# Attention scores from 64-row products: two heads side by side on the array, keys held without their zero blocks

## The chip, the cores and the metric

The kernel runs on one core of a Trainium2 chip. The metric is the device time of one execution in microseconds (us). A core has five engines that run at the same time and wait for each other through semaphores: TensorE (PE in the profile; its weight loads are listed apart as PEld), VectorE (DVE), ScalarE (ACT), GpSimd (POOL) and SyncE (SP, which here only issues DMAs).

## What is computed

The inputs are float32. The first half is an attention whose keys and values are first averaged over groups of 8 positions; the second half is a feed-forward block with an unusual activation over all 4608 positions.

```python
# q, k, v: (8 batches, 8 heads, 576 positions, 64)
k_p = k.reshape(B, H, 72, 8, 64).mean(axis=3)          # 72 pooled keys
v_p = v.reshape(B, H, 72, 8, 64).mean(axis=3)
scores = (1 / 8) * np.matmul(q, k_p.transpose(0, 1, 3, 2))
scores = scores - scores.max(axis=-1, keepdims=True)
attn = np.exp(scores); attn = attn / (attn.sum(-1, keepdims=True) + 1e-9)
x = np.matmul(attn, v_p)                               # heads joined: (4608, 512)
h = x @ w_in                                           # (4608, 2048)
sp = np.maximum(h, 0) + np.log1p(np.exp(-np.abs(h)))
out = (h * erf(sp)) @ w_out                            # (4608, 512)
```

## The kernel before, in words

**The work.** The 4608 rows of `x` are cut into 9 chunks (`ck`) of 512, and the feed-forward block runs chunk by chunk: products with `w_in` (L1004 for chunks 0 and 1, L948 with seven half-size products for the others), the activation on ACT and DVE, and products with `w_out` (L1062). These two lines and L948 are most of the kernel. The attention of a batch (`job`) is put between them, so that a chunk's rows of `x` are ready when the chunk starts.

**Attention of a batch.** The pooled keys of the four pairs of heads come into a tile `ks` (128 partitions x 4 pairs x 72): partitions 0 to 63 hold the channels of one head of a pair, partitions 64 to 127 those of the other. In batches 1 to 7 two ACT instructions (L654) copy them, with a factor of -1/64, into `kbd`, which has 144 columns for a pair: 72 of one head with zeros in the other head's rows, then 72 of the other. The zeros come from one memset at the start (L465). Batch 0 has a tile of its own for this, `kb0`.

**A full tile** (`softmax_tile`) is 128 queries of all 8 heads; a batch from 1 to 7 has 4 of them, 28 in all. The queries lie in `raw` as 128 partitions (two heads' channels) x 4 pairs x 128. Its scores are four products (L718), in two groups of two: the queries of a pair are the stationary operand (128 rows x 128 columns), `kbd` of that pair is the moving one (144 columns). Each group has a PSUM bank of its own. DVE then takes the extreme and subtracts it, ACT takes the exponential (as a sigmoid with a bias, so that the activation table of the feed-forward block serves), DVE and POOL normalise, TensorE turns the tile (L774, and L788 for the part that goes over 128), ACT and DVE split it into a high and a low part, and the products with the values follow (L898).

**A half tile** (`half_tile`) is what 576 leaves over: 64 queries, one for each of batches 1 to 7. Its four products (L821) have a stationary operand of 128 rows x 64 columns; two of them write partitions 0 to 63 of the bank and two write 64 to 127, one after the other in turn, so that each takes one half of the array's columns. It has the same chain behind it as a full tile, with L850 and L858 for the turning.

**The order.** Every operation is entered in a small planner (`Program`) with an engine, a cost in ns, a due time and the tiles that it reads and writes. The planner runs through them greedily and writes each engine's instructions in the order that it finds; for the start of the kernel a table (`FIRST`) gives the order by hand, as a list of operation numbers. Costs and due times set only the order: on the chip each engine takes its own list in sequence and waits on semaphores. The scores of a tile have a cost of 2 x 250 for each group, those of a half tile 2 x 250.

Of the kernel before, what the change touches and what calls it, by code (L numbers as in the profile page):

```python
# [11 lines left out]
F32 = mybir.dt.float32  # L12
# [8 lines left out]
POOL = 8  # L21
# [52 lines left out]
HALF_SCORES = 2  # L74
# [109 lines left out]
D137 A377 A376 A104 G142 G132 P1745 P407 P404 P1751 D345 D105 P1752 G385 D346 D108 D111 D405 P1753 P1746 P1747 A149 A141 A138 A148 A156 S380 S196 S168  # L184
S175 S382 S182 S549 S545 G386 G347 D408 D143 D406 P1754 P348 D409 D144 G139 G387 G389 P1755 P350 P1748 P426 P1756 D381 D427 A163 A349 A351 A410 D411
G145 G146 D428 A1757 D412 P358 P352 P1769 P1770 P1771 P355 P1772 G393 D150 D413 A353 A359 A356 D354 D360 D357 D151 G390 G414 G415 P1773 P429 P1774
P361 P419 P416 P1777 D430 P1778 P1775 P1779 P1780 P1781 P1782 A1758 S481 S459 D431 D383 D1759 G152 G170 G153 G391 A422 A420 A155 D1762 D157 A417 G424
A1760 A362 A162 A1763 D418 D158 D363 D423 D164 A432 D433 D421 D165 G1761 G1764 P1783 P1776 P1784 P1797 P1798 P1799 P463 P1800 P1801 P1802 P460 P1765
G177 G159 S189 S231 A1785 D434 G160 A166 G184 G167 A169 A1786 D464 D461 D465 D171 D462 D172 D435 D173 G436 D1787 A176 A191 G437 G174 D1790 P1767 P1803
P1805 P1806 P1807 P1808 P1766 A1788 D178 D179 D1789 A183 A198 A1791 A180 D185 G394 P1809 P438 G395 A439 G181 D186 D440 A398 A396 A187 A190 S273 S294  # L190
S329 S203 S259 S217 S322 S245 S210 S1969 S224 S252 S553 S266 S280 S238 P1810 P1768 P1811 P1804 P1812 P1793 P1825 P1826 P1794 P1827 D1792 D400 G188
G401 G205 A1813 D192 D397 D193 A197 D194 D402 D199 G195 G212 D399 D200 A1814 D201 A204 A466 G219 G202 D1815 A1816 G1817 D1818 P1795 P1828 P1829 P1830
P1831 P1833 D206 P1834 P1835 A211 D207 D213 P1836 P1832 P1837 P1838 P441 P1796 P1839 A226 A1819 A442 A444 D208 G546 A233 D214 D443 D445 G446 D467 A218
G209 P447 P1840 A215 D220 P1821 S287 S1970 S2071 S2038 S1936 S308 A448 D468 D1820 D449 G216 D221 P450 A1841 D469 D222 A451 G470 D452 G223 P1822 P453
P456 P1823 P1824 A1842 D471 A457 A454 D1846 D455 D458 D1843 A225 P475 P472 D227 P1853 A1847 A476 A478 G240 G554 G550 G547 G548 G1848 A473 A1844 D228
D477 D474 D479 A232 D234 A229 A239 P1854 G1845 G230 D235 D241 A261 A254 A246 A247 D242 G551 G236 D243 G555 G237 G244 P482 A1855 D248 D483 D484 D249
P1849 P1850 A253 G250 G552 G251 D255 P485 P1851 P1852 S2037 S557 S2004 S515 A1856 D486 D256 D487 A260 A488 D1860 D262 D1857 D489 D263 A1861 A275 A268
A1858 A267 G257 G480 G556 G258 G558 D490 D1862 D491 D269 G1859 P1867 P1868 D270 A274 A264 A282 A271 G265 D276 P516 P1863 D517 D277 D518 P519 A1869
S301 S2105 S2106 S563 S567 G272 G492 P497 G568 P1864 P1866 A498 A500 D520 D493 D278 D499 D521 D501 G564 G279 G565 G559 G502 G296 P494 P1865 A1870
D1871 D1874 A289 A495 A281 A1872 A1875 D496 D283 D1873 D284 A522 A288 D290 P1881 P1882 G1876 G560 D285 G286 D291 A295 A310 A562 D297 D523 A561 A302  # L200
A303 D298 D304 G292 G293 P1877 D524 P503 A1883 D299 P1878 D525 D305 G300 G306 G526 G566 A504 D505 S616 S2072 S2140 S2003 S2139 S594 S1935 S315 S2181
A1884 D527 G324 G307 D1885 P509 P506 P1880 P1879 A507 A317 A510 A1886 D1888 D511 D508 D1887 P1895 A1889 A309 G1890 A316 D311 G569 S571 G570 D318 A331
S2182 P1896 D312 G572 D319 A313 G573 A323 S575 G314 A320 D325 P512 G321 D326 P1891 A1897 D327 P528 G574 G328 P1892 A513 A529 D514 D530 G576 P531 P1893
G577 S579 A1898 G578 P595 A532 P1894 A534 D1899 G536 D533 G580 D535 A1900 D1902 P1917 A330 S646 G1901 D596 A1903 D597 D332 G1904 D333 P598 A1918 G581
P1919 G334 D599 G582 D600 G335 A601 S583 D602 P537 A1920 G1933 S668 P539 P1951 D603 D538 G584 D540 A1921 D604 G585 G605 G586 D606 P541 P543 D1952
G1934 P1905 A1922 D542 G1937 S690 A544 P607 A587 D1923 P610 P617 A589 A608 P620 D1926 P1906 A1924 D618 G1938 A611 D609 A613 A1941 G615 D612 P1953 D614
A1927 G1925 D621 D619 A1945 S742 D622 D588 G1939 A623 D590 G1942 A1943 D624 P1907 G743 A1954 D625 G744 P1985 D626 D1940 G627 A1955 G745 D628 D1947
D1944 D1946 P1912 G1948 D1908 S746 A1956 D1910 P629 G1928 P1929 A630 S1949 D1957 A1986 P632 P647 D1960 A633 A1958 S1909 P650 D631 G747 P1931 A635
S1911 A1913 D634 G637 D636 D648 G748 S1950 A1915 D651 P1987 G749 D649 D652 S750 A653 S1914 D654 S1916 G751 P1930 S754 D591 D655 A592 P2019 D656 D1959
A1961 D593 A1988 G657 G1967 D658 P1932 A1989 D1968 P1963 D1962 G1971 D2020 P669 A1990 G752 P672 G1972 D670 P2021 A1975 D1991 A1979 D1994 A1992 D673  # L210
G1973 D671 S791 G1976 D674 A1977 P1964 D1974 A675 D1978 D1981 D676 G1980 P638 A1995 P640 D1993 A639 P1965 D677 A641 D2022 G1982 D678 D2001 P2053 S1983
D2002 G753 A2023 D2005 G755 S1984 D2006 P1966 D2007 S2197 D2009 D2008 A2024 D2011 P642 D1996 S760 P644 A643 G2013 D2054 P1997 A2015 G2010 A645 D2025
P659 D2028 A2026 P662 P2055 G679 A660 G2012 A663 A665 D661 G2014 D664 G667 D666 D680 P684 P691 A685 D2016 A687 P694 G2035 D686 D688 P1998 D692 S2017
D695 D693 G689 D696 G2036 P681 A2029 P1999 S2018 A682 D2027 A697 S2198 D683 G2039 P2087 A2056
# [172 lines left out]
def moe_attention(ctx: ExitStack, tc: tile.TileContext, cst, qa, kl, vl, wi, wo, out):  # L387
# [3 lines left out]
    if wide:  # L391
# [6 lines left out]
             "s": 2, "m": 2, "z": 2, "bb": 1, "ks": 1, "vs": 1, "hs": 3, "y": 1, "f": 2, "gh": 3, "gl": 2}  # L398
# [62 lines left out]
    kbd = const.tile([P, NP, 2 * SP], F32, name="kbd")  # L461
# [3 lines left out]
    nc.gpsimd.memset(kbd, 0.0)  # L465
    KBD, VA, VB = (Kept() for _ in range(3))
    kb0 = loan(LENT_KB, [NP, 2 * SP]) if wide else None
    if wide:
        op("POOL", 600, T0 - 8, lambda: nc.gpsimd.memset(kb0.ap, 0.0), [], [kb0])
# [99 lines left out]
    def factors(ck):  # L569
# [25 lines left out]
        split(5, "B21", b21, x1)  # L595
        split(6, "B22", b22, x1)
        split(7, "T4", one, (d, 0))

    def job(ck, b, tiles, off, times, first, fresh):

        bank = lambda kind: Buf(banks, [P, 512], F32, "banks", ["banks", "att0" if ck == 0 else kind])

        KB, kb = (kb0, lambda: kb0.ap) if b == 0 and wide else (KBD, lambda: kbd)
# [587 lines left out]
```

## Time and profile before

| | us |
|---|---|
| median of 3 runs | 888.25 (887.3 to 888.77) |
| the profiled execution | 888.12 |
| its span in the trace | 886.3 |
| TensorE busy | 878.1 (99%) |
| ScalarE busy | 639.4 (72%) |
| VectorE busy | 604.5 (68%) |
| GpSimd busy | 303.5 (34%) |

The span is what the instructions cover, from the first to the last; the execution's own time is 1.8 us longer. A product's record lasts until its last result is out, and the next record begins well before that, so that the busy time of a TensorE line is not the time that it takes from the engine. What it takes is read from the starts: how long after one record's start the next can start.

### The profile page before, as it was taken

The page shows a single profiled execution, that of the slowest core. Times are in us where ns is not written, and L with a number is a line of the kernel's source. Part 1 is how long each engine was busy: PE and PEld are TensorE (multiplying, and loading weights), DVE is VectorE, ACT ScalarE, POOL GpSimd, SP SyncE. Part 2 cuts the span into 40 slices and gives each one's busy share as a digit, 9 for nine tenths or more (in the row PEclk, how much of TensorE's full clock was granted, in tenths as well). Part 3 has the DMA queues.
Part 4 walks back from the last instruction along what each step waited for, and adds up shares of the span by engine and source line. Part 5 has one row for each costly group of instructions (what it writes and reads, how often), then busy time and mean ns, then how long its engine had stood idle before and what let it go on. Part 6 is the DMA issues. An engine that isn't in the chain of part 4 may idle for free.

```text
span 886.3 us, 15343 instructions
## 1 busy us (share of the span) xinstructions
PE 878.1 (99%) x5431; PEld 783.6 (88%) x5431; DVE 604.5 (68%) x1251; ACT 639.4 (72%) x1045; POOL 303.5 (34%) x433
## 2 busy tenths in 40 slices
PE   8999999999999999999999999999999999999998
PEld 7988888888989999999899998999899998999996
DVE  7998868889876566567765767757756665664333
ACT  6999988768777676667667767576766866666664
POOL 2978886450445311313342324322510211001110
PEclk9999999999999999999999999999999999999999
DMA  9995523346776656655665468545755464546421
GB/s 340 358 387 176 190 99 130 142 170 234 250 250 214 216 178 228 211 179 189 246 213 181 150 222 277 201 145 195 241 172 167 166 214 166 167 166 214 167 84 48
DMA packets 65467, 176.05 MB, mean 199 GB/s; under 512 B 7152, under 2 KB 10992, under 8 KB 65392
## 3 DMA queue, kind: packets, MB, share of 16 engines
q1 hardware_dynamic: 65104, 174.69, 56.5%
q8 instruction: 43, 0.70, 0.3%
q10 hardware_dynamic: 288, 0.39, 0.1%
q14 instruction: 32, 0.26, 0.1%
HBM read 150.94 MB, written 24.12 MB: 198 GB/s over the span
## 4 chain that ended last, share of the span: by engine, by line
PE 91%; DVE 1%; ACT 0%; DMA 0%; issue 0%; DVEq 0%; ACTq 0%
PE banks L1062 43%; PE banks L948 32%; PE banks L1004 7%; PE banks L898 3%; PE banks L718 3%; PE banks L774 1%; PE banks L821 1%; PE banks L788 0%; DVE banks L496 0%; DMA out<-f 0%; PE banks L850 0%; ACT L1029 0%; ACT y L1029 0%; DVE wi L966 0%; DVE f L506 0%
## 5 line engine op out<-in xcount | busy, mean ns | idle before, releaser
L1062 PE MATMUL banks<-wo,gh 128*128 128x512 f32 x1154 | 365.0, 398 | 0.0
L948 PEld LDWEIGHTS banks<-t,wi 128*128 128x128 f32 x2352 | 304.3, 191 | 12.8 <-DVE hs L966 0.3
L948 PE MATMUL banks<-t,wi 128*128 128x256 f32 x2352 | 313.0, 283 | 0.1
L1062 PEld LDWEIGHTS banks<-wo,gh 128*128 128x128 f32 x1154 | 202.4, 189 | 31.7 <-issue 1.0
L1062 PE MATMUL banks<-wo,gl 128*128 128x512 f32 x577 | 224.9, 390 | 0.0
L1062 PEld LDWEIGHTS banks<-wo,gl 128*128 128x128 f32 x577 | 108.4, 188 | 24.5
L1029 ACT ACT_TABLE_LOAD x72 | 92.4, 1283 | 52.2 <-DVE hs L966 29.9
L966 DVE TENSOR_TENSOR wi<-wi,banks 128x256 f32<-128x256 f32 x168 | 67.5, 415 | 75.1 <-ACT wi L969 39.5
L1004 PE MATMUL banks<-t,wi 128*128 128x512 f32 (+1 forms) x480 | 97.7, 352 | 0.7 <-DVE y L1039 0.6
L638 POOL TENSOR_TENSOR raw<-raw 128x256 f32<-128x256 f32 (+1 forms) x60 | 47.5, 798 | 127.4 <-DMA raw<-vl 45.7
L1004 PEld LDWEIGHTS banks<-t,wi 128*128 128x128 f32 x480 | 78.8, 189 | 13.1 <-DVE y L1039 0.8
L1036 ACT ACTIVATE y<-y 128x1024 f32<-128x1024 f32 (+1 forms) x73 | 76.2, 1046 | 0.6
L1041 ACT CAST gh<-hs 128x512 fp32r<-128x512 f32 x72 | 44.5, 620 | 42.8 <-PE banks L1062 20.0
L1036 ACT ACT_TABLE_LOAD x57 | 73.1, 1283 | 1.0
L1046 DVE TENSOR_TENSOR gl<-hs,gh 128x512 fp32r<-128x512 f32 x48 | 35.9, 748 | 38.4 <-PE banks L1062 38.1
L1046 DVE TENSOR_TENSOR gl<-wi,gh 128x512 fp32r<-128x512 f32 x38 | 27.6, 728 | 47.8 <-PE banks L1062 42.7
L1046 POOL TENSOR_TENSOR gl<-hs,gh 128x512 fp32r<-128x512 f32 x24 | 31.5, 1312 | 79.9 <-PE banks L1062 44.2
L966 DVE TENSOR_TENSOR hs<-wi,banks 128x256 f32<-128x256 f32 x84 | 32.7, 417 | 32.8 <-PE banks L948 32.3
L1041 ACT CAST gh<-wi 128x512 fp32r<-128x512 f32 x56 | 34.4, 618 | 26.8 <-PE banks L1062 13.5
L1046 POOL TENSOR_TENSOR gl<-wi,gh 128x512 fp32r<-128x512 f32 x18 | 23.8, 1321 | 85.3 <-PE banks L1062 75.6
L1039 DVE TENSOR_TENSOR hs<-y,hs 128x512 f32<-128x512 f32 x72 | 50.6, 741 | 3.3 <-ACT y L1036 3.3
L1039 DVE TENSOR_TENSOR wi<-y,wi 128x512 f32<-128x512 f32 x56 | 40.8, 768 | 4.3 <-ACT y L1036 3.9
(169 smaller groups left out, 1237.8 us busy)
## 6 DMA issues: line engine op xcount, KB each, us to landing
wi<-w SPq DMA_DIRECT2D x168, 512.0 KB, 3.7
wi<-w SPq DMA_DIRECT2D x56, 256.0 KB, 4.1
raw<-vl SPq DMA_DIRECT2D x36, 256.0 KB, 3.7
wi<-wi SPq DMA_DIRECT2D x16, 512.0 KB, 7.5
wo<-wo SPq DMA_DIRECT2D x16, 512.0 KB, 7.3
w<-t SPq DMA_DIRECT2D x16, 512.0 KB, 2.8
raw<-qa SPq DMA_DIRECT2D x30, 256.0 KB, 4.1
raw<-kl SPq DMA_DIRECT2D x26, 288.0 KB, 4.3
```

What stands on the lines that cost most here:

```text
L638: op("POOL", gps(4 * size), prio, lambda: nc.gpsimd.tensor_add(t.ap[:, 0:4], t.ap[:, 0:4], t.ap[:, 4:8]), [t], [t])
L718: nc.tensor.matmul(o, raw.ap[:, p, :T], kb()[:, p, :], start=(pp == 0), stop=True, skip_group_check=True)
L898: nc.tensor.matmul(d, w, e, start=(i == 0), stop=(i == 3), skip_group_check=True)
L948: nc.tensor.matmul(dst(), weight(name, w, p), x[:, xl, p, :], start=(first and p == 0 and q == 0), stop=(p == 1 and q == 2), skip_group_ch ...
L966: return op("DVE", dve(HALF), prio, lambda: nc.vector.tensor_add(dst(), x(), b.ap[:, side]), reads + [b], writes)
L1004: nc.tensor.matmul(ph.ap[:, at:at + w], w_in[ft].ap[:, hl, P * p:P * p + P], xs[p].ap[:, x, at:at + w], start=(p == 0 and q == 0 and at == ...
L1029: nc.scalar.activation(y.ap[:, half(k)], hh[k].ap, AF.Softplus)
L1036: op("ACT", act(w), n + 1.9, lambda sl=sl: nc.scalar.activation(y.ap[:, sl], y.ap[:, sl], AF.Erf), own, own, funcs="sigmoid")
L1039: op("DVE", dve(TC), n + 1.9, lambda k=k: nc.vector.tensor_mul(g(k), y.ap[:, half(k)], hh[k].ap), [(y, k), hh[k]], [gs[k]], port=kept)
L1041: op("ACT", act(TC), n + 2.0, lambda k=k: nc.scalar.copy(gh[k].ap, g(k)), [gs[k]], [gh[k]], port=True, alt=("DVE", 0.52 * TC + 150, lambda ...
L1046: return e.tensor_sub(gl[k].ap, g(k), f32(gh[k].ap))
L1062: nc.tensor.matmul(o[t].ap[:, cols], g.ap[:, gs], w_out[ft].ap[:, w, cols], start=(ft == 0 and q == 0), stop=(ft == NJ - 1 and q == 2), sk ...
```

## The change

The scores of batches 1 to 7 are computed from `ks` itself, without `kbd`: its memset and the two ACT copies of each of these batches are gone, and `ks` has two buffers in place of one. `quad_tile` takes the place of `softmax_tile` (which stays for batch 0) and of `half_tile`. A head's product has 64 rows: the stationary operand is 64 rows x 128 queries, the moving one is that head's 72 columns of `ks`. The two heads of a pair lie in different halves of the partitions, so in different halves of the array's rows, and write different PSUM banks. A full tile has eight such products in place of four with 144 columns.

The 64 queries that are left over no longer have a tile of their own: they go with the full tile ahead of them, as two more "slots" of the same score tile, with eight products of 64 rows x 64 queries, one in each quarter of the array in turn. So seven of the 28 tiles have 6 slots, and 21 have 4. The chain behind the scores runs once over all slots (`s` is now 4 or 6 slots x 2 heads x 72), the sign that was in `kbd` is gone (maximum in place of minimum), and the factor 1/64 is in the activation's scale. What is turned, split and multiplied with the values is the same in number and size as before.

The planner's cost for the scores of a tile is now 122 for each slot and 330 once; the `FIRST` table is edited where operations are gone or joined. The diff, cut to its core:

```diff
-HALF_SCORES = 2
+QUAD, QUAD_IN = 122, 330
...
-D137 A377 A376 A104 G142 G132 P1745 P407 P404 P1751 D345 D105 P1752 ...
+D137 A377 A376 A104 G142 G132 P1745 P404 P1751 D345 D105 P1752 ...
...
-             "s": 2, "m": 2, "z": 2, "bb": 1, "ks": 1, ...
+             "s": 2, "m": 2, "z": 2, "bb": 1, "ks": 2, ...
...
-    kbd = const.tile([P, NP, 2 * SP], F32, name="kbd")
...
-    nc.gpsimd.memset(kbd, 0.0)
...
-                for r0, c0 in ((64, 0), (0, SP)):
+                for r0, c0 in ((64, 0), (0, SP)) if b == 0 else ():
...
-        def half_tile(k, qo, r):
...
-                for j in range(2):
-                    for g in range(2):
-                        o = ps.ap[T * g:T * g + T, 2 * SP * j:2 * SP * j + 2 * SP]
-                        nc.tensor.matmul(o, raw.ap[:, 2 * g + j], kb()[:, 2 * g + j, :], start=(j == 0), stop=True,
-                                         skip_group_check=True)
...
+        def quad_tile(k, qo, r, half):
+
+            slots = NP + (half is not None and 2)
...
+            ps = [bank("att") for _ in range(2)]
+
+            def scores():
+                for i in range(slots):
+                    for x, r0 in ((0, 64), (1, 0)):
+                        for y, c0 in ((0, 0), (1, 64))[:1 + (i >= NP)]:
+                            q, p = (raw.ap[:, i], i) if i < NP else (rawh.ap[:, 2 * y + i - NP], 2 * y + i - NP)
+                            nc.tensor.matmul(ps[x].ap[c0:c0 + q.shape[-1], SP * i:SP * i + SP], q[r0:r0 + 64], ks.ap[r0:r0 + 64, p],
+                                             start=(i == 0), stop=True, skip_group_check=True)
+
+            op("PE", QUAD * slots + QUAD_IN, r, scores, raws + [(ks, p) for p in range(NP)], ps, [s, m, z])
+            n = slots * SP
+            for x in range(2):
+                pv = lambda x=x: ps[x].ap[:, :n].rearrange("p (i k) -> p i k", k=SP)
+                op("DVE", dve(n), r + 0.4, lambda x=x, pv=pv: nc.vector.tensor_reduce(
+                    m.ap[:, :, x], pv(), AX.X, ALU.max), [ps[x]], [(m, x)])
...
+            op("ACT", act(2 * n) + 93, r + 0.8, lambda: nc.scalar.activation(
+                s.ap, s.ap, AF.Sigmoid, bias[0], 1.0 / 64.0), [s], [s], funcs="sigmoid")
```

On TensorE, in the middle of the kernel (batch 4), a full tile of before stands between products with `w_in` (L948) and with `w_out` (L1062):

```order
L948 MATMUL banks<-t,wi_4799 128x256 x6
L948 MATMUL banks<-t,wi_4821 128x256 x6
L948 MATMUL banks<-t,wi_4839 128x256 x6
L718 MATMUL banks<-kbd,raw 128x144 x4
L1062 MATMUL banks<-wo_1743,gh 128x512 x2
L1062 MATMUL banks<-wo_1743,gl 128x512
```

and a full tile of after in the same part of the program, where the lines of the feed-forward products are now L982 and L1096:

```order
L1096 MATMUL banks<-wo_1424,gh 128x512 x2
L1096 MATMUL banks<-wo_1424,gl 128x512
L832 MATMUL banks<-ks,raw 128x72 x8
L982 MATMUL banks<-t,wi_4591 128x256 x6
L982 MATMUL banks<-t,wi_4605 128x256 x6
```

Four products with 144 moving columns became eight with 72; the feed-forward products around them are of the same kinds.

The half tile of the same batch stands on TensorE before as

```order
L1062 MATMUL banks<-wo_611,gh 128x512 x2
L1062 MATMUL banks<-wo_611,gl 128x512
L821 MATMUL banks<-kbd,raw 64x144 x4
L948 MATMUL banks<-t,wi_5107 128x256 x6
L948 MATMUL banks<-t,wi_5121 128x256 x6
```

and after, with the full tile ahead of it, as

```order
L1096 MATMUL banks<-wo_1742,gh 128x512 x2
L1096 MATMUL banks<-wo_1742,gl 128x512
L832 MATMUL banks<-ks,raw 128x72 x8
L832 MATMUL banks<-ks,raw 64x72 x8
L982 MATMUL banks<-t,wi_4817 128x256 x6
L982 MATMUL banks<-t,wi_4846 128x256 x6
```

The place of its own that the half tile had on TensorE is gone; its eight products with 64 queries follow the full tile's eight at once.

## Rows read from the trace of the kernel before

**Rows 1.** The page: busy engines, TensorE's granted clock in 40 slices, the chain.

```profile
PE 878.1 (99%) x5431; PEld 783.6 (88%) x5431; DVE 604.5 (68%) x1251; ACT 639.4 (72%) x1045; POOL 303.5 (34%) x433
...
PEclk9999999999999999999999999999999999999999
...
PE 91%; DVE 1%; ACT 0%; DMA 0%; issue 0%; DVEq 0%; ACTq 0%
```

**Rows 2.** Busy time by stretch: start:end, its length, busy us of each engine.

```profile
0.00:30.00 30.00, 26.75 (x183) 23.24 (x184) 23.87 (x53) 22.60 (x83) 13.60 (x24) 1.00 0.96 352
30.00:60.00 30.00, 29.88 (x220) 27.95 (x220) 28.57 (x59) 29.08 (x50) 26.33 (x33) 1.00 0.95 360
60.00:100.00 40.00, 39.12 (x208) 32.36 (x207) 33.63 (x65) 36.96 (x59) 33.12 (x40) 1.00 0.57 201
100.00:870.00 770.00, 769.90 (x4769) 689.79 (x4768) 514.66 (x1072) 543.26 (x845) 230.41 (x339) 1.00 0.55 189
```

**Rows 3.** Scores by source line: records, duration ns min/median/max, first and last start, shape.

```profile
L718 PE MATMUL banks<-kbd,raw x224: 283/286/332, 30.5 to 735.1; 128*128 128x144 f32 x112
...
L821 PE MATMUL banks<-kbd,raw x56: 286/286/338, 84.4 to 749.7; 128*64 128x144 f32 x56
```

**Rows 4.** Timeline of PE at a full tile: start us, us, records merged.

```profile
413.94 2.32 PE L948 MATMUL banks<-t,wi 128*128 128x256 f32 x18
416.10 1.15 PE L718 MATMUL banks<-kbd,raw 128*128 128x144 f32 x8
416.98 0.72 PE L1062 MATMUL banks<-wo,gh 128*128 128x512 f32 x2
417.54 0.39 PE L1062 MATMUL banks<-wo,gl 128*128 128x512 f32 x1
```

**Rows 5.** Timeline of PE at the half tile of batch 5.

```profile
531.34 0.62 PE L1062 MATMUL banks<-wo,gh 128*128 128x512 f32 x2
531.80 0.39 PE L1062 MATMUL banks<-wo,gl 128*128 128x512 f32 x1
532.12 0.71 PE L821 MATMUL banks<-kbd,raw 128*64 128x144 f32 x8
532.76 0.73 PE L1062 MATMUL banks<-wo,gh 128*128 128x512 f32 x2
533.33 0.40 PE L1062 MATMUL banks<-wo,gl 128*128 128x512 f32 x1
```

**Rows 6.** Timeline of the weight loads there; in brackets the idle time before.

```profile
532.12 0.44 PEld L821 LDWEIGHTS banks<-kbd,raw 128*64 128x64 f32 x8 [0.36 <-DVE f L1095]
532.76 0.30 PEld L1062 LDWEIGHTS banks<-wo,gh 128*128 128x128 f32 x2 [0.20 <-issue]
```

**Rows 7.** The weight loads in the first 0.17 us of another half tile.

```profile
84.45 0.20 PEld L821 LDWEIGHTS banks<-kbd,raw 128*64 128x64 f32 x4 [0.35 <-issue]
```

**Rows 8.** Timeline of weight loads at batch 0's value products of 64 moving columns.

```profile
35.68 0.31 PEld L888 LDWEIGHTS banks<-eth,wo 128*128 128x128 f32 x2
35.91 0.30 PEld L889 LDWEIGHTS banks<-eth,wo 128*128 128x128 f32 x2
36.14 0.30 PEld L888 LDWEIGHTS banks<-eth,wo 128*128 128x128 f32 x2
36.36 0.30 PEld L889 LDWEIGHTS banks<-eth,wo 128*128 128x128 f32 x2
```

**Rows 9.** Weight loads by form: rows*columns; busy us, mean ns, idle before.

```profile
L718 PEld LDWEIGHTS banks<-kbd,raw 128*128 128x128 f32 x224 | 30.9, 189 | 1.6 <-DVE f L506 0.2
L898 PEld LDWEIGHTS banks<-etb,vb 96*64 96x64 f32 x60 | 8.2, 136 | 0.0
L821 PEld LDWEIGHTS banks<-kbd,raw 128*64 128x64 f32 x56 | 3.1, 136 | 2.1 <-issue 1.2 <-DVE f L1095 0.4 <-DVE wi L1039 0.4
```

**Rows 10.** The instructions that write `kbd`, from the view of that tile.

```profile
L654 ACT ACTIVATE kbd<-ks x14: 441/443/448, 29.5 to 629.3; 64x288 f32<-64x288 f32 x14
L465 POOL MEMSET kbd<- x1: 577/577/577, 0.9 to 0.9; 128x576 f32 x1
```

More of the change, by code (lines that the diff above doesn't have):

```diff
@@ L597, in factors @@
         split(7, "T4", one, (d, 0))
+    keys = {}
     def job(ck, b, tiles, off, times, first, fresh):
         bank = lambda kind: Buf(banks, [P, 512], F32, "banks", ["banks", "att0" if ck == 0 else kind])
[L603 removed]
+        KB, kb = kb0, lambda: kb0.ap
         base, due = times[0], times[-1] + (VAL_R0 if ck == 0 else VAL_R)
@@ new lines, in quad_tile, with low, third @@
+            op("PE", 322 if half else 55, r + 2.0, turn_rest, [bb] + [s] * bool(half), [pb], held)
+            def low(at, dst, src, tags, n):
+                op("ACT", act(n, True), r + 2.3, lambda: nc.scalar.copy(dst(0), src()), [pb], [(etb, (at, g, 0)) for g in tags])
+                op("DVE", dve(n), r + 2.4, lambda: nc.vector.tensor_sub(dst(32), src(), f32(dst(0))),
+                   [pb] + [(etb, (at, g, 0)) for g in tags], [(etb, (at, g, 1)) for g in tags])
+            def third(at, cs, T):
+                op("POOL", 1.666 * T + 161, r + 2.5, lambda: nc.gpsimd.tensor_scalar(
+                    out=etb.ap[64:96, :, cs], in0=f32(etb.ap[0:32, :, cs]), scalar1=1.0, scalar2=0.0,
+                    op0=ALU.mult, op1=ALU.add), [(etb, (at, g, 0)) for g in range(2)], [(etb, (at, 0, 2))])
@@ new lines, in quad_tile @@
+            for g in range(2):
+                low(k, lambda r0, g=g: etb.ap[r0:r0 + 32, g, cs], lambda g=g: pb.ap[32 * g:32 * g + 32, :P], (g,), P)
+            third(k, cs, P)
+            if half:
+                ch = slice(kh, kh + P // 2)
+                pr.skip(14)
+                pbh = lambda: pb.ap[:, 2 * P:].rearrange("k (j g t) -> k g j t", j=2, g=2)
+                four = lambda e: e.ap[:, :, ch].rearrange("k (g j) t -> k g j t", j=2)
+                op("ACT", act(2 * P, True), r + 2.3, lambda: nc.scalar.copy(four(eth), pbh()), [pb], [(eth, kh)])
+                op("DVE", dve(2 * P), r + 2.4, lambda: nc.vector.tensor_sub(four(etl), pbh(), f32(four(eth))),
+                   [pb, (eth, kh)], [(etl, kh)])
+                pr.skip(1)
+                low(kh, lambda r0: etb.ap[r0:r0 + 32, :, ch], lambda: pb.ap[:32, P:2 * P].rearrange("k (g t) -> k g t", g=2), (0, 1), P)
+                pr.skip(2)
+                third(kh, ch, P // 2)
@@ L869, in job @@
         at = 0
         for (qo, T), r in zip(tiles, times):
-            if T < P and not full:
-                half_tile(at, qo, r)
-            else:
+            if full:
                 softmax_tile(at, qo, T, r)
+            elif T == P:
+                quad_tile(at, qo, r, next(((at + P, q, rh) for (q, n), rh in zip(tiles, times) if n < P and q == qo + P * NP * P), None))
             at += T
```

154 lines of the change are left out of this document (75 added, 79 removed).

## The prediction

> **What bounds the kernel now.** I read the page first: TensorE is busy for 99% of the span, at the full granted clock in every slice (the 2.4 GHz level), and the chain that ended last is 91% TensorE [rows 1]. Then the busy time by stretch, to see whether that holds everywhere: from 100 to 870 us TensorE lacks 0.1 us of 770, while VectorE has 255 us idle and ScalarE 227. Before 100 us it lacks 3.3 us of the first 30, then 0.1 of 30 and 0.9 of 40 [rows 2]. So the end is set by the sum of what TensorE has to do. A step removed on another engine gains nothing by itself, and each 0.1 us that the scores take more or less on TensorE is 0.1 us of the kernel. The rest is therefore about TensorE's own pace at the scores.
>
> **A full tile now.** Its four products are 8 records (224 for 28 tiles) [rows 3]. The first starts at 416.10, and the run lasts 1.15 us with the last record's own 0.286, so seven steps take 0.864: 0.123 each, 0.98 us for the tile [rows 3, 4]. With 144 columns that is 0.85 ns a column; I estimate 72 columns at half, 0.061.
>
> **A half tile now.** Here two products stand in different halves of the array's columns. First to last start is 0.71 - 0.286 = 0.42 us for 8 records, where one after another they would need 7 x 0.123 = 0.86: they run two at a time, in four steps of 0.123, 0.49 us [rows 3, 5]. But the half tile takes more than that from the engine. The last product before it starts at 531.80 and takes its usual step of 0.23 (as 531.34 and 531.80 with two records of it show), so the engine could go on at 532.03. The third product behind it starts at 533.33; two steps of 0.23 back, the first had its effective start at 532.87. That is 0.84 us, 0.35 more than the steps. The loads show where it is: 0.36 us without a load ahead of the half tile's first, and 0.20 ahead of the first one behind it [rows 6]. The loads aren't brought forward over the change in how the array is cut; the engine runs empty, loads, and starts, once on the way in and once on the way out. I split the 0.35 into 0.15 in (532.03 to the first load at 532.12, and that load, 0.055) and 0.20 out.
>
> Scores of batches 1 to 7 now: 28 x 0.98 + 7 x 0.84 = 33.3 us.
>
> **A weight load's price.** Where a product streams only 64 columns, the loads come in pairs at 35.68, 35.91, 36.14 and 36.36: 0.112 us for a load of 128 columns, though two passes over 64 columns should take some 0.055 [rows 8]. So short products wait for their weights, 0.112 each. For a load of 64 columns the four loads of rows 7 lie within 0.20 - 0.136 = 0.064 us of each other, two by two: some 0.055 each, and loads for the two halves of the columns run at the same time. Does a load with half the rows take half the time? By the nearest rows, no: 96 rows x 64 columns take 136 ns, 128 rows x 64 columns take 136 ns, 128 x 128 take 189 [rows 9]. The columns count. The Trainium skill, "TensorE: Matmul & The Clock Gate", section "LDWEIGHTS (loading the stationary operand)", states the same down to fewer rows, that a load of 32 rows takes as long as one of 128; by this rule, which speaks against the change, the loads of 64 rows keep the price of full ones. No run here has shown a load of 64 rows yet.
>
> **A full tile after.** Sixteen records in place of 8, in two rows-halves that I expect to run side by side, as the two column halves do: 8 steps of two records. The moving part of a step is 0.061, its load of 128 columns 0.112, so the load sets the step. With the way in and out: 0.35, plus 0.055 because the first load has 128 columns where the half tile's had 64, plus 7 x 0.112, plus 0.061 for the last step = **1.25 us**, 0.27 more than now. There are 21 such tiles: +5.7 us. The end from below for the step is 0.061 (loads free), from above 0.224 (loads one after another); I take 0.112, because rows 7 show loads of two halves side by side and rows 9 show that the rows don't count. Were the moving parts of a pair not to overlap, the step would be 2 x 0.061 = 0.122, which changes little.
>
> **A tile with the half in it.** The same 1.25, then another cut of the array (quarters): a way in of 0.15, and 4 steps of 0.061 with four products at a time (a load of 64 columns, 0.055, hides under it), 0.24 us. Together 1.64 us in place of 0.98 + 0.84 = 1.82: -0.18, seven times, **-1.3 us**. The second change of cut is bounded by 0 (no cost) and 0.35 (a full one in and out): 1.0 us less to 1.4 us more in all.
>
> Sum on TensorE: +5.7 - 1.3 = **+4.4 us**.
>
> **All else, at nothing.** The two copies of the keys (14 x 0.443 = 6.2 us of ScalarE) and the memset (0.58 us on GpSimd at 0.9 us) go [rows 10]; neither engine is waited for. The chain behind the scores of the half tile (its own reductions, exponential and reciprocal) is joined with the full tile's; VectorE loses work that nobody waits for. The scores now need both PSUM banks at once instead of one after the other, and the 64 queries' DMA is issued earlier, past loads of values and weights on SP; both are covered, after 100 us, by a TensorE that never waits for them. If that cover is gone, it is in the first 100 us: there the joined tile of batch 1 comes earlier, onto a VectorE busy for 28.6 of 30 us from 30 to 60 [rows 2]. What TensorE lacks after 30 us is 1.0 us altogether, so I price this at +-1.
>
> **The rivals.**
>
> *A: a load of 64 rows takes half the time.* Then the moving part sets the step: 0.35 + 8 x 0.061 = 0.84 for a full tile, -0.14 x 21 = -2.9 us; with the half 0.84 + 0.39 = 1.23 in place of 1.82, -0.59 x 7 = -4.1. Together -7.0: 881.1 us, **faster**. The sum turns at a step of about 0.09 (0.112 gives +4.4 us and 0.061 gives -7.0; zero lies between in proportion). For it: the loads of two halves do overlap [rows 7], and the planner's cost in the diff, 122 ns for a slot of two pairs of records, is what such a step would give; that is a number of the program and not of the trace. Against it: rows 8 and 9. The Trainium skill, "TensorEngine Tiling (Array Packing)", section "Theoretical Speedup", gives up to twofold for two halves of the rows; by this rule the 0.98 of a tile would be 0.49 and the change of cut, which is this rival.
>
> *B: no running empty for halves of the rows.* The way in and out is known from halves of the columns alone. If the loads were brought forward here, a tile is 8 x 0.112 = 0.90 (-0.08 x 21 = -1.7 us), and one with the half 0.90 + 0.24 = 1.14 (-0.68 x 7 = -4.8): -6.5, 881.6 us. Against it: all seven half tiles run empty on both sides; rows 6 are one of them.
>
> *C: the loads of the two halves go one after another.* A tile is then 0.35 + 0.055 + 15 x 0.112 + 0.061 = 2.15 (+1.17 x 21 = +24.6), one with the half 2.15 + 0.15 + 16 x 0.06 = 3.26 (+1.44 x 7 = +10.1): +34.7, some 923 us. Against it: rows 7.
>
> **How the numbers follow.** The profiled execution took 888.12, the median of the runs shown is 888.25, so the difference of 0.13 is nothing to explain; I add to 888.25. The forecast is 888.25 + 4.4 = **892.6 us**. Its own range: the second cut (-1.0 to +1.4), the step at 0.122 in place of 0.112 (+2), the early stretch (+-1): 890.5 to 896.5. Chances: forecast 0.57, A 0.24, B 0.10, C 0.07, and 0.02 for a mixture near no change. The range that holds eight in ten has to take in A and B besides the forecast: 880 to 897; C is left out. This kernel's time can be told from no change by about 0.2%, 1.8 us. Slower by more: the forecast, nearly all of it, and C, 0.62; faster by more: A and B, 0.33; within: 0.05.
>
> **What the new profile would show.** In the timeline of TensorE a run of 16 records at the new line of the scores: by the forecast 7 x 0.112 = 0.78 us from first to last start, by A 0.43, by C 1.68. Ahead of it and behind it idle time of the loads as in rows 6; without that, B. The loads of 64 rows at 189 ns by the forecast, near 136 by A. In the joined tiles a second idle time of the loads between the products of 128 and of 64 queries. TensorE's waits after 100 us stay near nothing; if they grow by more than 1 us, the order or the chain of the larger tile costs something that I set at nothing. The forecast is wrong first of all if the step of a pair isn't 0.11.

## The result, and the profile after

The changed kernel takes 898.39 us (median, 896.81 to 899.41), the kernel before, run beside it, 888.1: a ratio of 1.0105 with a 95% interval from 1.0089 to 1.012. The change costs 10.3 us, where the prediction said 4.4. The sign was right, the size was not, and 898.39 lies beyond the upper end of the range.

The profiled execution took 899.05 us with a span of 897.3, 11.0 more than the 886.3 of before. The page shows nothing of this at first sight: TensorE is still busy for 99% of the span and makes up most of the chain that ended last. Busy time and chain from the page of after:

```profile
PE 887.8 (99%) x5711; PEld 783.9 (87%) x5711; DVE 603.7 (67%) x1223; ACT 629.4 (70%) x1014; POOL 299.1 (33%) x421
...
PE 88%; DVE 1%; POOL 1%; ACT 0%; issue 0%; DVEq 0%; ACTq 0%; POOLq 0%
```

**The scores.** The timelines of TensorE at a full tile (16 records) and at one with the 64 queries in it (32), in after; columns as in [rows 4]:

```profile
351.37 0.40 PE L1096 MATMUL banks<-wo,gl 128*128 128x512 f32 x1
351.70 1.12 PE L832 MATMUL banks<-ks,raw 64*128 64x72 f32 x16
352.74 1.69 PE L982 MATMUL banks<-t,wi 128*128 128x256 f32 x12
...
421.34 0.40 PE L1096 MATMUL banks<-wo,gl 128*128 128x512 f32 x1
421.67 1.53 PE L832 MATMUL banks<-ks,raw 64*128 64x72 f32 x32
423.12 2.05 PE L982 MATMUL banks<-t,wi 128*128 128x256 f32 x15
```

The weight loads at the full tile, with the idle time ahead of them, the first loads behind it, and the loads of all score products by source line (ns min/median/max):

```profile
351.70 0.97 PEld L832 LDWEIGHTS banks<-ks,raw 64*128 64x128 f32 x16 [0.37 <-issue]
352.74 1.48 PEld L982 LDWEIGHTS banks<-t,wi 128*128 128x128 f32 x12
...
L832 PEld LDWEIGHTS banks<-ks,raw x560: 129/188/188, 32.4 to 746.3; 64*128 64x128 f32 x149, 64*64 64x64 f32 x38
```

Sixteen loads of 188 ns fit into 0.97 us. First to last start is 0.97 - 0.188 = 0.78 us, seven steps of a pair at 0.112 each, which is the forecast's figure. The loads stand idle for 0.37 us on the way in; behind the tile they stand idle for 0.07 us only (352.67 to 352.74). Worked out as in [rows 5], from the last usual step ahead to the first behind, a full tile takes 1.25 us and a joined one 1.65; the forecast had 1.25 and 1.64.

**Where the 11 us are.** To find the rest I gave every product outside the scores its usual step by its number of moving columns (0.227 us for 512, 0.119 for 256, and so on, the same in every kernel), and added up by stretch what the starts in the trace show beyond that ("time lost"). Together with the time of the score blocks this closes:

| TensorE, us | before | after | difference |
|---|---|---|---|
| score blocks of batches 1 to 7 | 33.6 | 38.7 | +5.1 |
| first 30 us: batch 0's scores and time lost | 12.2 | 13.6 | +1.3 |
| 30 to 100 us: time lost | 3.0 | 4.6 | +1.6 |
| from 100 us: time lost | 6.4 | 9.5 | +3.1 |
| sum | | | +11.1 (span: +11.0) |

So the scores, 4.4 in the forecast, hold 5.1; three rows that I had put at nothing hold 6.0. Busy time of after by stretch (columns as in [rows 2]):

```profile
0.00:30.00 30.00, 26.66 (x172) 23.39 (x173) 21.95 (x50) 21.10 (x78) 11.42 (x21) 0.94 0.93 336
...
60.00:100.00 40.00, 38.07 (x197) 31.23 (x197) 33.95 (x58) 36.92 (x59) 32.26 (x38) 1.00 0.61 220
100.00:870.00 770.00, 769.59 (x4965) 681.28 (x4964) 512.09 (x1045) 528.75 (x810) 227.63 (x330) 1.00 0.55 189
```

From 60 to 100 us TensorE lacks 1.9 us, where it lacked 0.9 [rows 2]. In the first 30 us its clock was not full (0.94). After 100 us it lacks 0.4 us: the 3.1 us there are **not waits**. They are products that are themselves slower. Groups of TensorE by line and form, busy us and mean ns of one; before first, then after:

```profile
L1062 PE MATMUL banks<-wo,gl 128*128 128x512 f32 x575 | 224.3, 390 | 0.0
L1004 PE MATMUL banks<-t,wi 128*128 128x512 f32 x288 | 69.4, 392 | 0.0
```

```profile
L1096 PE MATMUL banks<-wo,gl 128*128 128x512 f32 x575 | 226.4, 394 | 0.0
L1038 PE MATMUL banks<-t,wi 128*128 128x512 f32 x288 | 70.9, 396 | 0.6 <-DVE etb L879 0.6
```

These lines are the same code with the same operands in both kernels, and each of these products takes 4 ns longer (the products with the high part, `gh`, do not: 398 ns before, 396 after). A timeline run of 24 of them makes the same visible in starts (before, then after):

```profile
103.02 5.61 PE L1004 MATMUL banks<-t,wi 128*128 128x512 f32 x24
```

```profile
106.53 5.75 PE L1038 MATMUL banks<-t,wi 128*128 128x512 f32 x24
```

Less the last record's own time and divided by 23, that is 227.0 ns a step before and 232.8 after.

### The profile page after: what moved, and what is told of

It reads as the page before. It is cut to its first block, busy times and chain, and to the rows that moved or that the text cites. A ratio compares the mean times of both kernels' runs of the same rounds, so it can differ in the third digit from the quotient of the medians.

```text
span 897.3 us, 15793 instructions
## 1 busy us (share of the span) xinstructions
PE 887.8 (99%) x5711; PEld 783.9 (87%) x5711; DVE 603.7 (67%) x1223; ACT 629.4 (70%) x1014; POOL 299.1 (33%) x421
## 4 chain that ended last, share of the span: by engine, by line
PE 88%; DVE 1%; POOL 1%; ACT 0%; issue 0%; DVEq 0%; ACTq 0%; POOLq 0%
PE banks L1096 42%; PE banks L982 31%; PE banks L1038 7%; PE banks L832 3%; PE banks L932 3%; PE banks L859 1%; PE banks L869 0%; DVE hs L1073 0%; DVE gl L1080 0%; PE banks L873 0%; ACT L1063 0%; POOL wo L509 0%; POOL wi L509 0%; POOL t L561 0%; ACT y L1063 0%
## 5 line engine op out<-in xcount | busy, mean ns | idle before, releaser
L1096 PE MATMUL banks<-wo,gh 128*128 128x512 f32 x1154 | 362.6, 395 | 0.2 <-POOL wo L509 0.2
L982 PEld LDWEIGHTS banks<-t,wi 128*128 128x128 f32 x2352 | 303.2, 189 | 13.3
L982 PE MATMUL banks<-t,wi 128*128 128x256 f32 x2352 | 312.6, 284 | 0.0
L1096 PEld LDWEIGHTS banks<-wo,gh 128*128 128x128 f32 x1154 | 202.7, 188 | 34.1 <-POOL wo L509 0.6
L1096 PE MATMUL banks<-wo,gl 128*128 128x512 f32 x577 | 226.9, 393 | 0.0
L1096 PEld LDWEIGHTS banks<-wo,gl 128*128 128x128 f32 x577 | 108.3, 188 | 24.7
L638 POOL TENSOR_TENSOR raw<-raw 128x256 f32<-128x256 f32 (+1 forms) x60 | 49.3, 824 | 113.6 <-DMA raw<-kl 32.1
L1080 POOL TENSOR_TENSOR gl<-hs,gh 128x512 fp32r<-128x512 f32 x21 | 27.2, 1295 | 96.0 <-PE banks L1096 67.3
L1080 POOL TENSOR_TENSOR gl<-wi,gh 128x512 fp32r<-128x512 f32 x15 | 19.4, 1295 | 90.6 <-PE banks L1096 78.8
L1063 ACT ACTIVATE y<-hs 128x512 f32<-128x512 f32 x72 | 41.5, 624 | 0.4
```

The source lines that it names most:

```text
L638: op("POOL", gps(4 * size), prio, lambda: nc.gpsimd.tensor_add(t.ap[:, 0:4], t.ap[:, 0:4], t.ap[:, 4:8]), [t], [t])
L982: nc.tensor.matmul(dst(), weight(name, w, p), x[:, xl, p, :], start=(first and p == 0 and q == 0), stop=(p == 1 and q == 2), skip_group_ch ...
L1063: nc.scalar.activation(y.ap[:, half(k)], hh[k].ap, AF.Softplus)
L1080: return e.tensor_sub(gl[k].ap, g(k), f32(gh[k].ap))
L1096: nc.tensor.matmul(o[t].ap[:, cols], g.ap[:, gs], w_out[ft].ap[:, w, cols], start=(ft == 0 and q == 0), stop=(ft == NJ - 1 and q == 2), sk ...
```

## The experiments

The first theory was the prediction's: the step of a pair of loads, 0.112, and the way in and out, 0.35. Rivals for the rest were the order that wrong planner costs make, the absent memset, and, after the first runs, the place of the tiles in SBUF, which the change moves because `kbd` is gone (2304 bytes a partition) and `ks` (a second buffer), `s`, `m`, `z` and `bb` have other sizes.

### Quarters for all queries

If the loads' columns set the step, loads of 64 columns should bring it to the moving part's 0.061. From the kernel after:

```diff
-                        for y, c0 in ((0, 0), (1, 64))[:1 + (i >= NP)]:
-                            q, p = (raw.ap[:, i], i) if i < NP else (rawh.ap[:, 2 * y + i - NP], 2 * y + i - NP)
+                        for y, c0 in ((0, 0), (1, 64)):
+                            q, p = (raw.ap[:, i, c0:c0 + 64], i) if i < NP else (rawh.ap[:, 2 * y + i - NP], 2 * y + i - NP)
```

> The changed kernel with all scores of batches 1 to 7 in quarters of the array (64 rows x 64 queries, four at a time) in place of halves of the rows; nothing else is touched. Theory (the step of a pair is set by the load of 128 columns, 0.112 us; a load of 64 columns costs half and hides under the product): a step of 0.062, a full tile 0.35 + 8 x 0.062 = 0.85 us instead of 1.25, a joined one 0.35 + 12 x 0.062 = 1.10 without the second idle time instead of 1.66: -8.4 - 3.9 = -12.3 us against the changed kernel, about 886. Rival (64-row loads cost 0.112 whatever their columns): steps stay at 0.112, full tiles at 1.25, about 897 to 898.

Measured: 886.01 us against 888.38 for before, ratio 0.9973 (0.9963 to 0.9982). It is faster than both kernels. Loads and products at a full tile of it, and its joined tile:

```profile
345.67 0.58 PEld L832 LDWEIGHTS banks<-ks,raw 64*64 64x64 f32 x32 [0.36 <-issue]
...
345.67 0.73 PE L832 MATMUL banks<-ks,raw 64*64 64x72 f32 x32
...
414.49 0.98 PE L832 MATMUL banks<-ks,raw 64*64 64x72 f32 x48
```

Thirty-two loads of some 133 ns lie in 0.58 us: seven steps in 0.45, 0.064 each, four loads side by side. A full tile takes 0.86 us, a joined one 1.12, all blocks 26.8 us (33.6 before, 38.7 after). Number of rows, of heads and of moving columns are those of after; the columns of a load are halved, and four products stand side by side in place of two. That separates the step from everything else in the change: with the same way in and out, the loads of 128 columns are what makes the scores of after slower than those of before. It also shows that TensorE's time is the kernel's: the blocks lose 11.9 us, the kernel 12.4 (898.39 to 886.01; some 1 us of this is the clock at the start, below).

### Row halves for the full tiles alone

The kernel before with 64-row products in the full tiles; half tiles and `kbd` stay, `ks` has two buffers, and the order around them is kept near that of before. The second buffer moves the tiles behind `ks`, from `hs` to `gl`, and the weights by 1152 bytes, to 128 beyond a multiple of 512; `t` stays where it was.

```diff
-            for g in range(2):
+                    for i in range(NP):
+                        for x, r0 in ((0, 64), (1, 0)):
+                            nc.tensor.matmul(pair[x].ap[:, SP * i:SP * i + SP], raw.ap[r0:r0 + 64, i], ks.ap[r0:r0 + 64, i],
+                                             start=(i == 0), stop=True, skip_group_check=True)
```

> The kernel before with the 64-row products for the full tiles alone: half tiles, their block diagonal and the two copies of the keys stay, the planner's cost of a full tile stays 1000. Theory A (the scores' own price is +0.27 us a full tile and what is beyond comes with the joined tile's longer chain): 28 x 0.27 = +7.6 us, 895.7, and TensorE's other waits as before. Rival B (what is beyond comes with scores that need two banks at once and a pair that gets out of step): the same +7.6 and 3 to 4 us more, 899 to 900, with runs of 16 records that last over 1.0 us from first to last start.

Measured: 899.5 us, ratio 1.0133 (1.0119 to 1.0147). Its time lost from 100 us is 9.2, that of after, and the same products are slower:

```profile
L1090 PE MATMUL banks<-wo,gl 128*128 128x512 f32 x575 | 226.4, 394 | 0.0
L1032 PE MATMUL banks<-t,wi 128*128 128x512 f32 x288 | 70.8, 396 | 0.0
```

So the order of after and the joining are not what makes the products slower. From 30 to 100 us the time lost outside the score blocks is 3.1 us, that of before. But its blocks take 42.5 us, where 28 x 1.25 and 7 x 0.84 make 40.9, and of the other 1.7 about 1.0 is a wait: the tile at 98.12 has its sixteen records in step, and behind it TensorE stands until VectorE is done with `s`. The remaining 0.7 is one tile in which a pair got out of step. The wait, then that tile with the ScalarE copy that runs beside it:

```profile
98.12 1.11 PE L720 MATMUL banks<-ks,raw 64*128 64x72 f32 x16
100.36 0.27 PE L886 MATMUL banks<-cst,bb 128*32 128x128 f32 x1 [1.13 <-DVE s L735]
...
155.44 0.44 PE L720 MATMUL banks<-ks,raw 64*128 64x72 f32 x2
156.15 1.11 PE L720 MATMUL banks<-ks,raw 64*128 64x72 f32 x14 [0.27 <-ACT hs L1045]
157.19 0.73 PE L1090 MATMUL banks<-wo,gh 128*128 128x512 f32 x2
...
155.51 0.59 ACT L1045 COPY hs<-banks 128x512 f32<-128x512 f32 x1 [0.88 <-POOL gl L1074]
```

In the tile at 155.44 two records start, the next ones wait, and the engine comes to a stop a second time: 1.95 us in place of 1.25. ScalarE copies out of a bank until 156.10, and the held products start at 156.15. After has three such tiles, 0.8 us in all (at 552.70, for one, 1.81 us).

The time is the one that my rival named (899 to 900), but not by the rival's cause: pairs out of step make 0.7 us here and not 3 to 4; the slower products (2.8 us) and the wait make up the rest.

### The planner's costs

```diff
-QUAD, QUAD_IN = 122, 330
+QUAD, QUAD_IN = 200, 450
```

> The changed kernel with the planner's cost of the scores at what the trace shows (200 a slot and 450 once, so 1250 and 1650, in place of 818 and 1062); the order after the hand-written table may move, the work stays the same. If the order that came from a wrong cost makes up the loss beyond the scores' own price (some 3 us after 100 us): 895 to 896. If not: 897 to 900, as the changed kernel.

Measured: 896.81 us, ratio 1.0098 (1.0085 to 1.0112), 1.6 below the median of after and the same as the lowest run of it. Its time lost is 9.3 us from 100 us on and 4.1 ahead of that from 30. All four of its runs were at a mean clock of 0.999 or more; those of after at 0.999 took 896.81 and 897.73. So costs near the measured blocks give no other result; the order that the lower costs made is not the cause.

### The memset put back

After, with a memset of nearly the same size (512 columns; `kbd` had 576) at the old place, on another tile that is written later:

```diff
+    nc.gpsimd.memset(vah.bitcast(F32), 0.0)
```

> The changed kernel with a memset of 512 floats on GpSimd at the place of the one that was removed, so that GpSimd starts as before. If the missing memset shifted the start and so cost TensorE its clock for 3.4 us there: no dip of the clock at the start in any run, about 1 us less in the median (897.3). If the dip is a matter of chance at each start: as the changed kernel, dips in some runs, 896.8 to 899.4.

Measured: 898.2 us, ratio 1.0115 (1.01 to 1.0131). No difference to after in the time. Its four runs were all at a mean clock of 0.999 or more, as I expected for a memset that matters to the clock at the start (below), but the median is not 1 us lower, as I expected with it. So this run doesn't settle whether the two are connected.

### The tiles moved, nothing else

The kernel before, every instruction and the order the same, with two tiles that nobody uses: 256 bytes a partition ahead of all pools, 1152 behind `ks`. Then `t` begins 256 bytes beyond a multiple of 512 and the tiles from `hs` to `gl` and the weights 384 beyond, as in after. In before all these begin at multiples of 512.

```diff
+    const.tile([P, 64], F32, name="pad")
...
+        if t == "ks":
+            pool("pad", 1).tile([P, 288], F32, name="pad2")
```

> The kernel before, its instructions and their order untouched, with two unused tiles (256 and 1152 bytes a partition) that move the others as the change does: the feed-forward's tiles, which all began at a multiple of 512 bytes, begin 256 (t, raw) or 384 (hs, gh, gl, weights) bytes beyond one. Theory L (the place of the tiles makes the feed-forward products slower, as all kernels with two buffers of ks have shown: 232.8 ns a step at the first chunks' products instead of 227.7, 120.5 instead of 120.3, 230.6 instead of 230.2): about +2.2 us, 890.5, and 232 to 233 ns at L1004's line. Rival (those steps come from the scores or the order): as before, 888.4, 227.7 ns.

Measured: 893.14 us, ratio 1.0051 (1.0037 to 1.0066). The time lost from 100 us on is 9.1 us (6.4 before). The place of the tiles alone costs 4.5 us by the medians. Three of its five runs were at a mean clock of 0.998 or less, the profiled run among them, so that some 1 us of this is the start (below); the two others took 891.66 and 892.73, 3 to 4 us more than before. I had expected 890.5: the effect is there, at about twice the size.

### After and quarters with the old places

The converse: the order of instructions of after, and of quarters, with `s`, `bb`, `ks` and `vs` put behind the weights and `m` and `z` to the front, so that `t`, the tiles from `hs` to `gl` and the weights begin at multiples of 512 bytes again.

```diff
-    pools = {t: pool(t, n) for t, n in sizes.items()}
+    last = ("s", "bb", "ks", "vs")
+    pools = {t: pool(t, sizes[t]) for t in ("m", "z", *(t for t in sizes if t not in ("m", "z") + last))}
...
+    pools.update({t: pool(t, sizes[t]) for t in last})
```

> The changed kernel, its instructions and their order untouched, with the small tiles (m, z ahead; s, bb, ks, vs behind the weights) placed so that all of the feed-forward's tiles begin at a multiple of 512 bytes again. Theory L: 2 to 2.5 us less than the changed kernel, about 896. Rival: 898.4.

> The kernel with all scores in quarters (886.0), with the tiles placed as in the run beside it. Theory L: 883.5 to 884, 4.5 us below the kernel before. Rival: 886.

Measured: after with the old places 893.67 us, ratio 1.0056 (1.0042 to 1.0069); quarters with them 883.63, ratio 0.9944 (0.9931 to 0.9956). The second is the fastest version found, 5 us below before. After with the old places gained more than expected (about 896), and its five runs were all at a mean clock of 0.999 or more: of the 4.7 us between the medians some 1 us is the clock. The products of the first, by form, are back where they were:

```profile
L1098 PE MATMUL banks<-wo,gl 128*128 128x512 f32 x575 | 224.2, 390 | 0.0
L1040 PE MATMUL banks<-t,wi 128*128 128x512 f32 x288 | 69.5, 392 | 0.7 <-DVE etb L881 0.7
```

and the time lost from 100 us on is 6.2 us (6.7 in quarters with the old places, 9.2 in quarters). What is left of after's loss, 5.7 us by the spans, is the scores (+5.0) and the 30 to 100 us (+1.0).

### Column halves in the kernel before

To price the way in and out by itself: each full tile's product of before as two of 64 queries in the two halves of the columns. The stream of a tile stays 8 steps (two products at a time), but all of the places at which a full tile's scores stand now change the cut of the array.

```diff
+                        for c0 in (0, 64) if not full else ():
+                            nc.tensor.matmul(ps.ap[c0:c0 + 64, 2 * SP * pp:2 * SP * pp + 2 * SP], raw.ap[:, p, c0:c0 + 64], kb()[:, p, :],
+                                             start=(pp == 0), stop=True, skip_group_check=True)
```

> The kernel before with each of the full tiles' products (128 rows, 144 moving columns) issued as two of 64 queries in the two halves of the array's columns, order untouched: the step of a pair stays 0.122, and what is added is the way in and out of the cut array, once for each run of these products on TensorE (39 in the trace: 17 tiles whole, 11 in two pieces). Theory (the array runs empty on both sides of a cut, 0.35): 39 x 0.35 = +13.7 us, 902. Rival (the 0.35 of the half tiles came from waits of their own): within 2 us of before.

Measured: 901.09 us, ratio 1.0141 (1.0125 to 1.0156): +12.5 us for 39 places, 0.32 each (two of its four runs were at a mean clock of 0.997; by the two others, 900.0 us, it is 0.30). Loads of a tile and behind it:

```profile
351.71 0.93 PEld L719 LDWEIGHTS banks<-kbd,raw 128*64 128x64 f32 x16 [0.36 <-issue]
352.84 1.49 PEld L953 LDWEIGHTS banks<-t,wi 128*128 128x128 f32 x12 [0.20 <-issue]
```

The 0.20 of [rows 6] now stands behind every place; ahead of it the loads are idle for 0.36 us where the product in front has 512 columns and for 0.13 where it has 256, at the same price. A full tile of it takes 1.33 us in place of 0.98. Splitting an otherwise unchanged product over the array is a loss of 0.30 to 0.35 a place here, though its halves overlap.

### Which tiles' place

Three kernels from before, again with every instruction and the order the same, that move one group each: `t` by 256 bytes; `hs` to `gl` by 384; the weights by 384.

```diff
+        if t in ("t", "raw"):
+            pool("pad" + t, 1).tile([P, 64], F32, name="pad" + t)
```

```diff
+        if t == "hs":
+            pool("pad", 1).tile([P, 96], F32, name="pad")
...
+    pool("pad2", 1).tile([P, 32], F32, name="pad2")
```

```diff
+    pool("pad", 1).tile([P, 96], F32, name="pad")
     weights = pool("weights", 1)
```

> The kernel before, every instruction and the order the same; a tile of 256 bytes a partition that nothing uses stands ahead of the feed-forward block's input t, another behind it, so that t alone lies 256 bytes off (7.75 to 8.0 ns of its place in the kernel with all tiles moved), all other tiles begin at the same distance from a multiple of 512 bytes as before. Theory T (the moving operand's place counts): the products with w_in of 512 moving columns (L1004 before) take 232.7 ns a step in place of 227.7, those with w_out stay at 230.2; 217 steps after 100 us and as much again ahead of it where they are of 512 columns: +1.1 to +2 us, 889.5 to 890.5. Theory W (the weights' place counts): no change, 888.3.

(The bracket in this one is a slip and means nothing.)

> The kernel before, instructions and order the same; only the tiles from hs to gl (what ScalarE, VectorE and GpSimd compute between the two products, with the stationary operands of the products with w_out) lie 384 bytes off. Theory T: no change of any step, since no moving operand is among them: 888.3. Rival (the stationary operand's or the other engines' place counts): the step of the products with w_out rises from 230.2 to 230.7, +0.7 us, 889.

> The kernel before, instructions and order the same; only the weights lie 384 bytes off. They are the moving operand of the products with w_out and the stationary one of those with w_in. Theory T: the products with w_out go from 230.2 to 230.7 ns a step (+0.7 us, 889), those with w_in stay at 227.7. Theory W: those with w_in go to 232.7 as well, +1.1 to +2 us more, 890 to 891.

Measured, with 888.31 us for before:

| moved | us | ratio (95%) | time lost from 100 us, us |
|---|---|---|---|
| `t` | 888.25 | 0.9997 (0.9988 to 1.0006) | 6.4 |
| `hs` to `gl` | 891.0 | 1.0029 (1.0018 to 1.0039) | 8.6 |
| weights | 892.55 | 1.0048 (1.0035 to 1.006) | 9.9 |

By form, the products with `w_out` and with `w_in` where `hs` to `gl` moved, then where the weights moved:

```profile
L1067 PE MATMUL banks<-wo,gl 128*128 128x512 f32 x575 | 226.5, 394 | 0.0
L1009 PE MATMUL banks<-t,wi 128*128 128x512 f32 x288 | 69.6, 393 | 0.0
```

```profile
L1063 PE MATMUL banks<-wo,gl 128*128 128x512 f32 x575 | 226.4, 394 | 0.0
L1005 PE MATMUL banks<-t,wi 128*128 128x512 f32 x288 | 70.7, 396 | 0.0
```

Both moves cost more than any of my expectations for them (889 for `hs` to `gl`, 890 to 891 for the weights). My theory that the moving operand's place decides falls: the products with `w_in` go from 392 to 396 ns when their stationary operand, the weights, is moved, while moving their moving operand, `t`, does nothing. The products with `w_out` have the stationary operand in `gh` and `gl` and the moving one in the weights; those with `gl` slow down when either is moved alone (390 to 394 ns), those with `gh` keep their 398. `t` was moved by 256 bytes only, its distance in after, so that no run tells what 128 or 384 would do to it. It doesn't add up: all moved (893.14 us) cost no more than the weights alone. For the weights and the tiles from `hs` to `gl`, 384 bytes beyond a multiple of 512 is not special: the row halves have them 128 beyond and show the same 394 and 396. Why such a place makes the products slower is open.

## Why the prediction was wrong

**Right: what bounds the kernel.** From 100 to 870 us TensorE lacks 0.4 us of 770 in after, and what quarters take from its blocks (11.9 us) comes off the kernel (12.4, some 1 us of it the clock). The sum over TensorE's starts, against before, closes to 0.1 us on the span of after, of quarters and of the row halves, and to 0.3 us on that of after with the old places; that it closes is bookkeeping and shows only that no term was left out.

**Right: the load sets the step.** 0.112 was measured in after, 0.064 with loads of 64 columns. The Trainium skill, "TensorE: Matmul & The Clock Gate", section "LDWEIGHTS (loading the stationary operand)", says that columns and not rows make the time of a load; the loads of 64 rows by 128 columns (188 ns, where those of 128 rows have 189 [rows 9]) agree. Rival A, with its 0.061 for 64 rows, is out; a step of that size came with fewer columns (0.064 in quarters).

**Right: the way in and out.** The loads stand idle for 0.37 us ahead of the tile, so rival B is out; column halves gave the price by itself. C is out with the sixteen loads in 0.97 us. The second cut in the joined tile, bounded by 0 and 0.35, took about what I set: 1.65 us for the tile against 1.64. Its loads, those with 128 columns and those with 64 (two windows of the timeline):

```profile
421.66 0.97 PEld L832 LDWEIGHTS banks<-ks,raw 64*128 64x128 f32 x16 [0.36 <-issue]
...
422.71 0.33 PEld L832 LDWEIGHTS banks<-ks,raw 64*64 64x64 f32 x16
```

From the last start of the first group (422.63 - 0.188 = 422.44) to the first of the second are 0.27 us where a step is 0.112, so some 0.15 for the cut. Two signs that I had named came out smaller: the idle time of the loads is 0.07 us behind a full tile, not 0.20, and 0.08 at the second cut (422.63 to 422.71). The price is in the starts; this idle time is no measure of it.

**Mis-sized: the sum of the scores**, +5.1 for +4.4. Of the 0.7 missing, all is in the three tiles where a pair got out of step (0.8). The pair's two heads write different PSUM banks, and I had written that needing both at once is covered by a TensorE that never waits. It isn't quite: in these tiles the second head's product comes a little later than the first's, and the engine stops once more. That the bank is the cause is read from the trace (in the row halves the held products start 0.05 us after ScalarE's copy out of a bank ends), and wasn't tried. The sum's small slips change nothing: rival B comes to 881.75, and the forecast's own range goes up to 897.0 by its own terms.

**The step that failed: "All else, at nothing".** Three things were in it.

- *The place of the tiles*, +3.1 us in the trace from 100 us on. I took from the change what it does to instructions, and from the absent `kbd` that a memset and 14 copies go. That every tile behind it gets another address, and that an address could change the pace of more than 800 unchanged products (575 with `gl`, 288 with `w_in`), I hadn't considered. With the old places the same instructions take 893.67 us, 1.1 from the forecast of 892.6. Of those 4.7 us less some 1 us is the clock; the rest, 3 to 4 us, is the place, and carries most of the error of 5.8. The remainder is the scores (0.7) and the next point.
- *The stretch from 30 to 100 us*, +1.6 (I had +-1). With the old places it is +1.0, so that some 0.6 is the place again. For the rest, the cover there was thin, as I wrote, and it went. TensorE's waits in that stretch, in after (us in total, times, longest):

```profile
PE banks L1038 <- DVE etb L879: 0.6, 1, 0.6
PE banks L1038 <- DVE y L1073: 0.6, 1, 0.6
PE banks L932 <- DVE t L950: 0.5, 2, 0.3
PE banks L1096 <- POOL wo L509: 0.2, 1, 0.2
```

  The wait for `y` was there before; that for `etb`, the split values of the attention, is new. It stands in each of the six kernels with a joined tile (0.6 or 0.7 us) and in none of the others, and the six lose 4.0 to 5.1 us in this stretch, those of before with moved tiles 3.0 to 3.5. That the joining as such costs this is not shown: the row halves, which keep the half tiles, have a new wait of another kind here (the 1.1 us for `s`) and with it lose as much, some 4.2 us. The row halves alone are enough to use up the cover; which step does it in after is open.
- *The clock at the start*, +1.3 in the profiled run. The first scores in before and in after, then busy time in steps of 2 us, in after:

```profile
7.79 2.20 PE L718 MATMUL banks<-wi,hs 128*128 128x144 f32 x16 [2.12 <-ACT wi L654]
...
7.97 3.87 PE L720 MATMUL banks<-wi,hs 128*128 128x144 f32 x16 [1.99 <-DMA hs<-qa]
...
6.00:8.00 2.00, 0.03 (x1) 0.06 (x1) 0.90 (x2) 0.65 (x3) 0.00 (x0) 1.00 0.95 318
8.00:10.00 2.00, 2.00 (x10) 2.00 (x11) 0.47 (x2) 1.12 (x5) 0.00 (x0) 0.57 1.05 400
10.00:12.00 2.00, 2.00 (x11) 1.88 (x11) 1.16 (x3) 2.00 (x14) 0.00 (x0) 0.58 1.01 399
```

  TensorE waits 2.0 us for the first queries; then its clock is granted at about half for most of 4 us (the 1.2 GHz level), and 10 products fit where 18 did before. The change is not needed for it: before idles as long there and keeps its full clock in its profiled run, the kernel with the moved tiles, which keeps the memset and the old order, shows the same fall (0.998 in its profiled run), and the runs of after split, two at a mean clock of 0.997 and 0.998 (899.05 and 899.41 us), two at 0.999 (897.73 and 896.81). A run of before beside the first experiments has a low mean clock too (0.998, 890.55 us). So I take it for chance, which is argued and not shown. It puts about 1 us into the median of after.

**The range** ended at 897. It took in the other prices of the scores, but no price for a cause outside them.

## What to carry to other kernels

- A product that is split over parts of the array pays for the change of cut (0.30 to 0.35 us here, in and out) and, while short, for the columns of its weight load: half the rows gave a step of 0.112, half the columns as well 0.064. With few moving columns cut the columns too, and put as many products as there are into one stay.
- A change that adds, drops or resizes a tile moves every tile behind it. Compare the places of the large operands before and after, and compare the mean time of products that weren't changed: 390 against 394 ns over 575 records is nearly the whole sign of 3 to 4 us here. Two runs with an unused tile tell it apart from the change itself.
- Where TensorE never waits, add up starts against a usual step by kind. It tells a slower step from a wait, which busy shares don't. Look for waits behind each block before its time is put down to the block: in the row halves about 1 us of the blocks' sum was a wait of what follows.

## What the runs showed of the hardware that was not expected

- The same product of 512 columns takes 227.0 or 232.8 ns a step by where its operands lie in SBUF. With the weights and the tiles from `hs` to `gl` at multiples of 512 bytes it is the lower figure, with them 384 bytes beyond the higher; 128 bytes beyond, the mean of a record is the higher one as well (396 ns against 392). Moving `t` by 256 bytes gave no difference (888.25 against 888.31 us). On the whole kernel it is up to 4.2 us (892.55 against 888.31, the weights alone moved) with not an instruction changed.
- Loads for the four quarters of the array run side by side: 32 loads of some 133 ns in 0.58 us.
- Two products in the two row halves start 7 ns apart in nearly every pair; where the second is held up, the tile pays 0.1 to 0.7 us more in the cases named above (1.81 and 1.95 in place of 1.25).
